# Unread products of eight columns on TensorE, at the start of a DeltaNet and feed-forward kernel

## The chip, the cores and the metric

The kernel runs on one core of a Trainium2 chip. A core has a matrix engine (TensorE, PE in the profile, with its weight loads shown as PEld), a vector engine (DVE), a scalar engine (ACT), a general engine (GpSimd, POOL) and a queue engine that issues transfers (SP). They work side by side and wait for each other through semaphores. Each of them carries out its own list of instructions in order; the list lies in memory, and an instruction queue brings it to the engine (q8 in the profile for TensorE). The metric is the device time of one launch in microseconds.

## The reference

Two layers stand one behind the other. The first is a delta rule over a sequence, for 4 batches and 8 heads, 768 steps and a head size of 48; the second is a feed-forward layer with exact GELU on 3072 tokens, 384 columns and 2048 hidden columns.

```python
k_n = k / (np.linalg.norm(k, axis=-1, keepdims=True) + 1e-06)
for t in range(S):
    y[:, :, t] = q_t @ state
    v_old = state.T @ k_t
    state = state + beta_t * outer(k_t, v_t - v_old)
x = y.transpose(0, 2, 1, 3).reshape(B * S, H * D)
h = x @ w_in
g = 0.5 * h * (1.0 + erf(h / sqrt(2)))
out = g @ w_out
```

All inputs are float32 but for the two weights of the feed-forward layer, which come as 64-bit floats and are decoded to 32 bits by the kernel.

## The kernel before

The sequence is cut into 12 chunks of 64 steps. A unit is one chunk of two batches (a = 0 or 1), with its 8 heads, so that 128 rows are filled: 64 steps of the one batch and 64 of the other. Inside a chunk the recurrence becomes a triangular system: K times K transposed, scaled by beta and by the norms of K, is eliminated in blocks of 32, the inverse is applied to V less the state's part, and the chunk's outputs and the next state follow from it.

The first four units (chunks 0 and 1, `first` in the code) are started by hand: within `by_hand` (L1201 to L1299) all five engines keep the order in which the code issues. For the work behind it a planner sorts the steps by due times written out in a list; there DVE and POOL keep that order, and PE keeps it where a chain of dependencies is laid.

What TensorE does in the part written by hand, in its order:

- For each of the four units, the transposition of K (L419, tile psT): four matmuls against the identity `ident`, after the unit's K has landed. ACT copies the result out as Kt (L420).
- In between and behind, the diagonal 32x32 products of K with itself (`diagonals`, L487, tile psD): 64 matmuls per unit in the profile's count, with 64 weight loads. The order is: transposition of unit 0, of unit 1, diagonals of unit 0, transposition of unit 2, diagonals of unit 1, transposition of unit 3, diagonals of unit 2, the signs of two chunks (L1195, psB, transpositions of beta), diagonals of unit 3. ACT copies each group out as `diag` (L489).
- The remaining products of K with itself (`grams`, L440, psG), once for each of the four units, and the signs of the other ten chunks.
- For each of the four units, the transposition of Q (L419 with `x` = 1), the copy by ACT, and then `queries` (L440, psG): Q times K transposed, which waits for that copy.
- The same for the units of chunks 2 and 3, then joins, solves and so on.

A float32 product appears in the profile as two weight loads and two matmuls, a transposition as one of each.

DVE meanwhile computes the norms of K (L345, L346), their roots (L390 to L396) and the factors from beta and the norms (L324 to L328), turns the factors (L498), turns all four units' diagonals at once (`flip`, L508), scales them (L513, with XM, which POOL made from the turned factors at L501) and eliminates row by row (L523 to L530). Then come the turns back (L539, L543), the joins of the 32x32 blocks (L578 on PE, L589 on DVE) and the decoding of the first weights (L255 to L282).

PSUM tiles come from pools by tag. The tag "mlp" has two buffers that are used in turn; the first tiles with it in the kernel before are `psY` of the first unit (L811), used behind the elimination.

## Time and profile before

| | us |
|---|---|
| median of 3 runs | 625.35 |
| the runs | 626.43, 625.1, 625.35 |
| the profiled execution | 626.68 |
| its span, first to last instruction | 624.9 |
| PE busy in it | 602.5 (96%) |
| DVE busy | 440.1 (70%) |
| ACT busy | 241.4 (39%) |
| POOL busy | 212.6 (34%) |

The span is cut into stretches by the views of the profile; times in them are microseconds from its start. A group of matmuls in the timeline is written with its line, output and input tiles, its shape, and its count. Brackets at the end of a row hold the idle time of the engine ahead of the group, and what ended it: another engine's instruction, a transfer, or "issue", which is time in which the engine waited for nothing that the profile shows. The chain that ended last is followed back from the last instruction: at each step to what released it, or to the instruction before it on the same engine. The row PEclk gives the granted TensorE clock as a share of the full one; the matmuls' own durations can be read beside it.

### The profile page before, as it was taken

How to read it: one execution, taken by the hardware profiler on the slowest of the kernel's cores; microseconds unless marked ns; L12 is line 12 of the kernel's file. 1: busy time of each engine (PE TensorE's matmuls, PEld its weight loads, DVE VectorE, ACT ScalarE, POOL GpSimd, SP SyncE). 2: the span in 40 equal slices, each digit the busy share in tenths (PEclk: the TensorE clock that was granted, in tenths of full speed). 3: DMA queues.
4: the chain of work that ended last, by engine and by line, in shares of the span. 5: the costliest groups of instructions: out<-in, count | busy, mean ns of one | idle time of the engine just before them, and what ended most of it. 6: DMA issues, size and time to landing. Idle time of an engine off the chain costs nothing.

```text
span 624.9 us, 19704 instructions
## 1 busy us (share of the span) xinstructions
PE 602.5 (96%) x8358; PEld 537.7 (86%) x8358; DVE 440.1 (70%) x811; ACT 241.4 (39%) x546; POOL 212.6 (34%) x316
## 2 busy tenths in 40 slices
PE   5768999999999999999999999999999999999997
PEld 4657786776899998998899998899998899988997
DVE  6999899999967697774859755859745947332532
ACT  3576877625443264224451134451134222044200
POOL 4045002100379821687222885222885200000000
PEclk9996999999999999999999999999999999999999
DMA  9793775002423452353123533013421001010011
GB/s 134 164 294 118 174 179 149 17 10 40 72 38 49 77 93 37 57 115 39 16 43 55 95 70 39 13 29 52 79 50 17 12 3 27 3 24 1 0 27 26
DMA packets 159576, 39.64 MB, mean 63 GB/s; under 512 B 151168, under 2 KB 154368, under 8 KB 159488
## 3 DMA queue, kind: packets, MB, share of 16 engines
q1 hardware_dynamic: 156816, 37.34, 30.9%
q10 hardware_dynamic: 2672, 1.03, 0.9%
q8 instruction: 66, 1.08, 0.7%
q14 instruction: 22, 0.18, 0.1%
HBM read 33.62 MB, written 4.72 MB: 61 GB/s over the span
## 4 chain that ended last, share of the span: by engine, by line
PE 81%; DVE 14%; issue 2%; DMA 1%; ACT 1%; SPq 0%; DVEq 0%
PE psX L966 13%; PE psY L1032 11%; PE psY L966 9%; PE psX L1032 9%; PE psV L1032 6%; PE psZ L1032 6%; PE psZ L966 4%; PE psV L966 4%; DVE tmp L528 3%; DVE Nu L530 3%; PE psK L732 3%; PE psO L933 3%; PE psH L915 2%; PE psY L822 2%; PE psU L792 2%
## 5 line engine op out<-in xcount | busy, mean ns | idle before, releaser
L377 POOL TENSOR_TENSOR n<-n,half 128x16 f32<-128x16 f32 x10 | 31.4, 3138 | 180.1 <-DVE n L375 130.0
L530 POOL TENSOR_TENSOR Nu<-Nu,tmp 128x30 f32<-128x30 f32 (+14 forms) x120 | 65.0, 541 | 9.4
L528 POOL TENSOR_TENSOR tmp<-Nu 128x30 f32<-128x30 f32 (+14 forms) x120 | 62.4, 520 | 9.4
L1032 PE MATMUL psX<-xT,w_in_sb 128*128 128x256 f32 (+1 forms) x288 | 62.6, 346 | 0.0
L966 PE MATMUL psX<-w_out_sb,G 128*128 128x192 f32 x320 | 56.1, 329 | 0.0
L966 PEld LDWEIGHTS psX<-w_out_sb,G 128*128 128x128 f32 x320 | 52.2, 190 | 0.7
L1032 PEld LDWEIGHTS psX<-xT,w_in_sb 128*128 128x128 f32 x288 | 47.9, 190 | 5.4
L915 PE MATMUL psH<-xT,w_in_sb 128*128 128x256 f32 x192 | 44.7, 387 | 0.7 <-ACT G L1015 0.5
L933 PE MATMUL psO<-w_out_sb,G 128*128 128x384 f32 x128 | 43.9, 490 | 0.0
L851 DVE TENSOR_TENSOR V<-psY,y 64x192 f32<-64x192 f32 (+1 forms) x60 | 21.3, 355 | 31.0 <-PE psY L834 27.0
L915 PEld LDWEIGHTS psH<-xT,w_in_sb 128*128 128x128 f32 x192 | 36.2, 192 | 7.9 <-ACT G L1015 2.3
L1060 DVE TENSOR_TENSOR psY<-psY,pu 128x512 f32<-128x512 f32 x20 | 14.0, 700 | 40.5 <-PE psY L1032 39.9
L1032 PE MATMUL psY<-xT,w_in_sb 128*128 128x256 f32 (+1 forms) x192 | 41.5, 345 | 0.0
L1015 ACT COPY xT<-psX 128x768 f32<-128x768 f32 x9 | 7.2, 799 | 79.8 <-PE psX L892 79.8
L1015 ACT COPY pu<-psZ 128x512 f32<-128x512 f32 x40 | 23.5, 587 | 37.3 <-PE psZ L1032 35.0
L933 PEld LDWEIGHTS psO<-w_out_sb,G 128*128 128x128 f32 x128 | 23.6, 190 | 14.1
L1032 PEld LDWEIGHTS psY<-xT,w_in_sb 128*128 128x128 f32 x192 | 32.1, 191 | 3.5
L1015 ACT ACTIVATE G<-G 128x512 f32<-128x512 f32 x40 | 25.2, 631 | 21.0 <-DVE G L1068 20.8
L1068 DVE TENSOR_TENSOR G<-psY,pu 128x512 f32<-128x512 f32 x20 | 13.8, 691 | 22.2 <-PE psY L1032 21.5
L1015 ACT ACTIVATE G<-psY 128x512 f32<-128x512 f32 x20 | 11.9, 596 | 45.3 <-PE psY L1032 45.3
L966 PE MATMUL psY<-w_out_sb,G 128*128 128x192 f32 x160 | 28.1, 329 | 0.0
L966 PE MATMUL psZ<-T,pu 128*128 128x192 f32 x160 | 28.1, 329 | 0.0
(207 smaller groups left out, 1370.2 us busy)
## 6 DMA issues: line engine op xcount, KB each, us to landing
Kp<-in_k_dram SPq DMA_DIRECT2D x76, 96.0 KB, 3.2
w_out_sb<-in_moe_w_in_dram SPq DMA_DIRECT2D x24, 256.0 KB, 4.0
V<-in_v_dram SPq DMA_DIRECT2D x48, 96.0 KB, 3.1
w_raw<-in_moe_w_out_dram SPq DMA_DIRECT2D x12, 384.0 KB, 7.4
out_dram<-o_sb SPq DMA_DIRECT2D x40, 96.0 KB, 2.2
Qp<-in_k_dram SPq DMA_DIRECT2D x64, 32.0 KB, 2.3
G<-in_moe_w_out_dram SPq DMA_DIRECT2D x4, 384.0 KB, 5.1
Qp<-in_q_dram SPq DMA_DIRECT2D x96, 16.0 KB, 2.0
```

What stands on the lines that cost most here:

```text
L377: nc.gpsimd.tensor_tensor(flat, flat, half, op=ALU.pow)
L528: rows_on.tensor_tensor(tmp, nu[:, j + 1:, j:j + 1].to_broadcast([128, n, j]), nu[:, j:j + 1, 0:j].to_broadcast([128, n, j]), op=ALU.mult)
L530: rows_on.tensor_tensor(nu[:, j + 1:, 0:j], nu[:, j + 1:, 0:j], tmp, op=ALU.add)
L732: nc.tensor.matmul(u.psK[HALF[p], r, j, :], lhsT=u.Kt[rows, p, j, :], rhs=SQ[rows, u.a, p ^ r, j, 0:w], start=True, stop=True)
L851: nc.vector.tensor_tensor(dst, src, pairs(u.y[at_], s), op=ALU.add)
L915: nc.tensor.matmul(psH, lhsT=w_in_sb[:, f // 2, m, f % 2 * 128:(f % 2 + 1) * 128], rhs=xTs[c][:, m, :], start=(m == 0), stop=(m == NM - 1))
L933: nc.tensor.matmul(u.psO, lhsT=G[:, u.a, f, :], rhs=w_out_sb[:, f, :], start=(f == 0), stop=(f == NF - 1))
L966: nc.tensor.matmul(ps_, lhsT=lhs[:, f, :], rhs=rhs[:, f, :], start=first and f == 0, stop=f == FH - 1, skip_group_check=not first)
L1015: i = fn(*args, **kw)
L1032: nc.tensor.matmul(ps_[:, i], lhsT=lhs[:, f // 2, f % 2 * 128:(f % 2 + 1) * 128], rhs=rhs, start=first and i == 0, stop=True, skip_group_c ...
L1060: nc.vector.tensor_tensor(L1["Y1"], L1["Y1"], L1["pu"][:, 0], op=ALU.add)
L1068: nc.vector.tensor_tensor(half(1, 1), shaped(L1["Y1"]), shaped(L1["pu"][:, 0]), op=ALU.add)
```

## The change

A helper `unread` is added. It takes a tile with the tag "mlp" and issues n products of a 32x8 slice of the identity with the same slice, all into the same 8x8 corner of that tile. Nothing reads the tile. Each product has 8 weight columns and 8 moving columns over 32 rows and is two weight loads and two matmuls. The helper is called with 38 ahead of the loop over the first units, so ahead of the first transposition of K, and with 4 in each of the four rounds of the loop that transposes Q, between the transposition and `queries`. That makes 54 products, 216 instructions, all on TensorE. Nothing else is changed.

```diff
+    def unread(n):
+
+        psI = ps.tile([128, 512], F32, tag="mlp", name="psI")
+        for _ in range(n):
+            nc.tensor.matmul(psI[0:H, 0:H], lhsT=ident[0:HB, 0:H], rhs=ident[0:HB, 0:H],
+                             start=True, stop=True)
+
...
         ns[c] = n0[:, c * NA:(c + 1) * NA]
+    unread(38)
     for u in first:
         squares(u, n0[:, u.t], nc.gpsimd if u.t == 1 else nc.vector)
         transposed(u, (0,))
...
         if u.c == 1:
             for x in sums_[5 * u.a:5 * u.a + 5]:
                 sum_of_squares(*x)
+        unread(4)
         queries([u])
     for a in range(NA):
         fetch_q(tiles[2, a])
```

## The prediction

> **What bounds the kernel now.** I read the page first: its slices and the chain that ended last.

> ```profile
> span 624.9 us, 19704 instructions
> ...
> PEclk9996999999999999999999999999999999999999
> ...
> q8 instruction: 66, 1.08, 0.7%
> ...
> PE 81%; DVE 14%; issue 2%; DMA 1%; ACT 1%; SPq 0%; DVEq 0%
> ```

> PE carries 81% of the chain, DVE 14%. Then I read busy time by stretches, to see where each of them does so (columns: stretch, length, then busy time with counts of PE, PEld, DVE, ACT, POOL, then clock and DMA).

> ```profile
> 67.00:150.00 83.00, 82.46 (x920) 62.39 (x918) 77.05 (x142) 49.87 (x140) 4.79 (x2) 1.00 0.35 85
> 150.00:240.00 90.00, 89.99 (x1547) 82.17 (x1540) 72.05 (x121) 38.50 (x79) 49.11 (x71) 1.00 0.42 66
> 240.00:250.00 10.00, 8.98 (x231) 8.50 (x230) 6.24 (x14) 4.48 (x9) 2.75 (x1) 1.00 0.25 32
> 250.00:350.00 100.00, 100.00 (x1612) 91.65 (x1615) 73.30 (x133) 34.71 (x71) 51.68 (x76) 1.00 0.34 56
> ```

> From 67 us on PE hardly ever stands still, so the end moves with the time at which PE gets there and with any stop after it. The one large stop is the 1.02 us at 240 to 250. Before 67 us the chain lies on DVE: from the flip of the diagonals (L508) at 14.95, through the elimination, to the join for which PE waits at 66.87. The change sits ahead of this, so the start of the chain matters:

> ```profile
> 12.01 0.27 PE psD L487 x10
> 12.28 1.36 issue
> 13.63 0.90 PE psD L487 x46
> ...
> 14.55 0.38 ACT diag L489
> ...
> 14.95 1.98 DVE Nu L508
> ```

> PE stands still for 1.36 us in the middle of the fourth group of diagonal products, waiting for no semaphore. DVE had been ready before the flip, since its previous instruction ended at 13.85:

> ```profile
> 13.64 0.21 DVE L498 STREAM_TRANSPOSE gt<-gm 128x32 f32<-128x32 f32 x1
> 14.95 1.97 DVE L508 STREAM_TRANSPOSE Nu<-diag 128x1024 f32<-128x1024 f32 x1 [1.10 <-ACT diag L489]
> ```

> So at most 1.1 us can be won there. PE's timeline tells what the stop is:

> ```profile
> 11.94 0.34 PE L487 MATMUL psD<-Kt 48*32 48x32 f32 x10
> 13.63 0.80 PE L487 MATMUL psD<-Kt 48*32 48x32 f32 x54 [1.36 <-issue]
> 14.37 2.40 PE L440 MATMUL psG<-Kt 48*64 48x64 f32 x74
> 17.37 1.76 PE L440 MATMUL psG<-Kt 48*64 48x64 f32 x54 [0.60 <-issue]
> ```

> **The change, part by part.** *38 products ahead of the first transposition.* A product is two weight loads and two matmuls, so 152 instructions. No row has this shape. Per load and matmul the nearest are psB (128 weight and 32 moving columns), 1.27 us for 10 or 127 ns; psJ at the same slow pace (32 and 32, two row groups in turn), 1.95 for 64, so 60 in each group; psD, four tiles at once, 14. A straight line through the first two gives 27 ns for 8 and 8 columns; bounds 14 and 127. 76 pairs take 2.05 us (1.1 to 9.7). They wait only for the identity, ready at 1.48, and so end at about 3.6; the first transposition waits for its K load until 4.47. Its price is nothing; if that cover went (127 ns) they would end at 11.2.

> *Four products behind each transposition of Q.* 8 pairs, 0.22 us, in the 0.67 us for which PE waits for ACT's copy (four gaps between 21 and 31). Hidden; without the cover 0.9 us of PE in a stage where DVE's elimination runs until 39.6 and PE idles another 2.06 us before 38.10. Nothing. No DMA, ACT, DVE, POOL or SP instruction is added or moved. The five unread tiles take turns with other "mlp" tiles, first used at 50.5 by PE itself: nothing.

> *What moves: the block edges.* With 152 instructions in front, the edges fall at the old numbers 41, 297 and 553 instead of 193, 449 and 705; with all 216, that of 7617 falls at 7401 and 7657.
> Number 41 stands in the first diagonal group, at 7.09. By the first fetch's 4.62 us (same loads under way) its block is there at 11.71; number 297, the beginning of the third group, was run at 10.76, so that group starts 0.95 late. Crossing there asks for the block of 553; between the rows 4.62 and 3.73 I take the middle, 4.18, because the loads thin out at 13 us. It is there at 15.89. Number 553 is the first instruction of the very last product of the fourth group (553 to 556), which the rest reaches at about 13.7. The flip began 0.80 after number 553 (14.15 to 14.95), so it now begins at 16.69: **1.74 later**. With 3.73 twice it is 0.40 later, with 4.62 twice 2.18. The other input of the elimination, the factors, is only 0.3 late (the signs move from 11.58 to 12.5) and stays ahead. What is late next is DVE's whole elimination, the decode behind it, and PE's join at 66.87; PE idles only 0.36 and 0.48 in that stretch, so I pass on all of it.

> *The late stop.* The new edges 7401 and 7657 are 242.56 and 246.05 (247.07 less the stop): 3.49 us apart, against 4.04 in the row. But the request runs ahead behind slow matmuls: between 4033 and 4289, another pair of edges, only 2.71 us passed without a stop, and eight slow matmuls stand ahead of 7381. I take 0.2 us of stop as left, **0.82 won**; bounds 0 and 1.02.

> *Sum.* +1.74-0.82=+0.92; ends +0.40-1.02=-0.62 and +2.18. The profiled execution took 626.68 (span 624.9 and 1.78 around it) and would take 627.60; it lies 1.33 above the median, 625.35, which becomes 626.27 (624.73 to 627.53).

> **Rivals.**
> *Faster: the last product comes in time.* If the edge falls at least four instructions later, or its block arrives by 12.6, only the third group is late: without any stop the fourth would end at 14.20-1.59=12.61, now at 13.56, and the flip starts at 14.31, 0.64 earlier; with the late stop's 0.82, 623.89. It decides at four instructions. For it: a single product is cut off. Against it: my count is exact at three stops.
> *Slower: new stops later.* Stretches of 256 that now begin at an edge and pass quickest are 7913 to 8169 (2.11 us) and 9449 to 9705 (2.10). If the request does not run ahead there, each costs 4.04-2.1=1.9: one makes 628.2. Slow matmuls stand ahead of both, which speaks against it.
> *The products are slow.* At 127 ns the first transposition moves from 4.47 to 11.2 and the second by 5: about 630.
> *Nothing moves:* PE has room for more, and the stops have another cause: 625.35.
> *The clock.* The slices give full clock in the first 34 us, but 48x64 matmuls last 315 ns there and 64x48 ones 308 in the stage at 0.50, against 220 behind 60 us: PE is slow until about 34. If the products woke it, number 41 would come up to 0.5 earlier and the end at 625.8; the blocks would still be waited for. [...]

> **How the numbers follow.** About 0.2% (1.25 us) is what a measurement of this kernel can tell from no change. Forecast 0.48 (0.27 of it within 0.2%, 0.21 slower, as its range goes to 627.53); faster rival 0.22 (0.20 faster, 0.02 within); new stops 0.12; slow products 0.05; nothing 0.08; clock 0.05. That makes 0.20 faster, 0.42 within, 0.38 slower. The time is the forecast's, 626.27. The range reaches to the faster rival and past the forecast's upper end towards the new stops: 623.7 to 628.0.

> **What would show it.** PE: 76 pairs end near 3.6; a stop before the third diagonal group and another two pairs ahead of the end of the fourth; L508 near 16.7; the join near 68.6; no 1.0 us stop at 245. Wrong, if L508 starts before 14.95, if stops keep their old matmuls, or if PE stops after 67 us where it did not.

## The result and the profile after

The changed kernel takes 628.06 us (median of 6 runs, 626.82 to 628.61), the kernel before 625.63 us beside it (6 runs, 625.1 to 626.43). The ratio is 1.0035, with a 95% interval of 1.0022 to 1.0048: slower by 0.35%, or 2.2 us (1.4 to 3.0). The prediction had +0.92 us, a ratio of 1.0015: the direction was right, the size less than half of what was measured. It gave a slowdown of more than 0.2% a chance of 0.38, less than the 0.42 for a time within 0.2%. Its range, 623.7 to 628.0, was set on the median of 625.35 known then; by the ratio the changed kernel stands at 627.5 on that base, inside the range, while the median of 628.06 lies just past its end.

The profiled execution of the changed kernel took 626.82 us, only 0.14 more than the 626.68 of the kernel before: it is the quickest of its runs, and that of the kernel before lies above all six of the runs beside it. So one pair of profiles hides most of the difference, and below three profiles of each kernel are read side by side. First the page of the changed kernel (span; granted clock in 40 slices; TensorE's instruction queue with packets, MB and share; the chain that ended last).

```profile
span 625.1 us, 19920 instructions
...
PEclk9985999999999999999999999999999999999999
...
q8 instruction: 66, 1.08, 0.7%
...
PE 80%; DVE 15%; issue 2%; ACT 1%; DMA 1%; SPq 0%; DVEq 0%
```

There are 216 instructions more and the same 66 packets. Then the busy time by stretches (PE, PEld, DVE, ACT, POOL with counts, then clock, DMA share and GB/s).

```profile
67.00:150.00 83.00, 82.36 (x876) 61.99 (x878) 77.05 (x142) 49.88 (x140) 4.79 (x2) 1.00 0.36 86
150.00:240.00 90.00, 90.00 (x1588) 82.19 (x1580) 71.95 (x122) 38.49 (x79) 48.91 (x70) 1.00 0.41 67
240.00:250.00 10.00, 10.00 (x240) 9.64 (x239) 6.28 (x13) 5.11 (x12) 2.90 (x1) 1.00 0.24 31
250.00:350.00 100.00, 99.31 (x1594) 90.90 (x1595) 74.19 (x134) 34.68 (x71) 51.44 (x75) 1.00 0.34 56
```

The 1.02 us that PE stood still between 240 and 250 are gone. In the next stretch, which was full, 0.69 us have come up. The start is read in PE's timeline of the changed kernel.

```profile
1.53 2.05 PE L1205 MATMUL psI<-ident 32*8 32x8 f32 x76 [1.53 <-POOL ident masks.py:199]
4.32 1.09 PE L419 MATMUL psT<-ident,Kp 128*128 128x128 f32 x4 [0.73 <-DMA Kp<-in_k_dram]
...
11.31 0.88 PE L487 MATMUL psD<-Kt 48*32 48x32 f32 x64 [0.41 <-issue]
12.12 0.42 PE L1195 MATMUL psB<-ident,w_in_sb 32*128 32x32 f32 x2
12.47 0.88 PE L487 MATMUL psD<-Kt 48*32 48x32 f32 x62
14.88 0.32 PE L487 MATMUL psD<-Kt 48*32 48x32 f32 x2 [1.53 <-issue]
```

The 76 pairs take 2.05 us and end ahead of K, which PE still waits for. The third group of diagonals (x64) starts behind a stop of 0.41, and the fourth is cut into 62 matmuls and 2: its last product alone waits for 1.53 us. The chain that ended last, of the same kernel, runs through that cut and on into DVE.

```profile
12.54 0.81 PE psD L487 x52
13.35 1.53 issue
14.88 0.33 PE psD L487 x2
...
15.23 0.38 ACT diag L489
...
15.64 1.96 DVE Nu L508
```

DVE's timeline says what the flip (L508) had to wait for. It was ready at 13.92, and ACT's copy of the cut group kept it for 1.72 us, where it was 1.10 before.

```profile
13.71 0.21 DVE L498 STREAM_TRANSPOSE gt<-gm 128x32 f32<-128x32 f32 x1
15.64 1.95 DVE L508 STREAM_TRANSPOSE Nu<-diag 128x1024 f32<-128x1024 f32 x1 [1.72 <-ACT diag L489]
```

Behind 244 us PE's timeline of the changed kernel has no stop in the products of L834 (that with 21 and 11 matmuls before), but a wait for DVE seven microseconds later.

```profile
244.40 0.54 PE L834 MATMUL psY<-V,Kp 64*48 64x48 f32 x32
...
251.77 1.76 PE L732 MATMUL psK<-SQ,Kt 48*64 48x112 f32 x64 [0.69 <-DVE SQ L841]
```

### The profile page after: what moved, and what is told of

Its sections match the earlier page's. It is cut to its first block, busy times and chain, and to the rows that moved or that the text cites. A ratio compares the mean times of both kernels' runs of the same rounds, so it can differ in the third digit from the quotient of the medians.

```text
span 625.1 us, 19920 instructions
## 1 busy us (share of the span) xinstructions
PE 609.2 (97%) x8466; PEld 544.2 (87%) x8466; DVE 440.6 (70%) x811; ACT 241.1 (39%) x546; POOL 212.4 (34%) x316
## 3 DMA queue, kind: packets, MB, share of 16 engines
q8 instruction: 66, 1.08, 0.7%
## 4 chain that ended last, share of the span: by engine, by line
PE 80%; DVE 15%; issue 2%; ACT 1%; DMA 1%; SPq 0%; DVEq 0%
PE psX L966 12%; PE psY L1032 11%; PE psY L966 9%; PE psX L1032 9%; PE psV L1032 6%; PE psZ L1032 6%; PE psV L966 4%; PE psZ L966 4%; DVE Nu L530 3%; DVE tmp L528 3%; PE psK L732 3%; PE psO L933 3%; PE psH L915 2%; PE psU L792 2%; PE psQ L752 2%
## 5 line engine op out<-in xcount | busy, mean ns | idle before, releaser
L851 DVE TENSOR_TENSOR V<-psY,y 64x192 f32<-64x192 f32 (+1 forms) x60 | 21.3, 355 | 30.4 <-PE psY L834 26.4
L933 PEld LDWEIGHTS psO<-w_out_sb,G 128*128 128x128 f32 x128 | 23.6, 190 | 14.1
```

The source lines that it names most:

```text
L851: nc.vector.tensor_tensor(dst, src, pairs(u.y[at_], s), op=ALU.add)
L933: nc.tensor.matmul(u.psO, lhsT=G[:, u.a, f, :], rhs=w_out_sb[:, f, :], start=(f == 0), stop=(f == NF - 1))
```

## The experiments

Four moments are compared throughout, each from one profiled execution: the start of the flip (L508); the join that PE waits for near 67 us (L578, psJ from Zf and XM); the products psK (L732) near 251, from their first weight load, as their distance from that join; and the end of the last matmul, as its distance from psK. "New stop" names a stop of PE that waits for no semaphore and that the kernel before does not have, by the number of the recorded PE instruction. Ratios are to the kernel before, run beside each; one without a ratio ran once.

| kernel | ratio, 95% interval | profile | flip | join | psK less join | end less psK | new stop behind 67 us |
|---|---|---|---|---|---|---|---|
| before | 1 | 626.68 | 14.95 | 66.86 | 184.69 | 369.89 | - |
| before again (e5) | 1.0004, 0.9992 to 1.0016 | 628.62 | 14.32 | 66.43 | 187.19 | 369.85 | - |
| before, third (e11) | - | 626.07 | 14.16 | 66.62 | 184.38 | 369.91 | - |
| after | 1.0035, 1.0022 to 1.0048 | 626.82 | 15.64 | 67.58 | 184.16 | 369.93 | none |
| after again (e1) | 1.0040, 1.0026 to 1.0055 | 628.69 | 16.85 | 68.65 | 184.19 | 370.68 | 8385: 0.67 |
| after, third (e10) | - | 628.77 | 16.95 | 68.80 | 184.23 | 370.55 | 8385: 0.54 |
| only the 38 (e2) | 1.0053, 1.0034 to 1.0072 | 629.38 | 16.70 | 68.62 | 184.36 | 371.21 | 9921: 1.15 |
| only the fours (e3) | 1.0016, 1.0005 to 1.0027 | 626.97 | 14.42 | 66.55 | 184.15 | 371.11 | 12481: 1.05; 7617, now ahead of L822: 0.31 |
| 37 and fours (e4) | 1.0017, 1.0005 to 1.0030 | 625.83 | 14.35 | 66.71 | 184.22 | 369.74 | none |
| only 64 (e6) | 1.0008, 0.9998 to 1.0017 | 626.64 | 15.22 | 67.13 | 184.44 | 369.91 | none |
| 54 behind Q (e7) | 1.0048, 1.0029 to 1.0067 | 628.43 | 14.14 | 68.50 | 184.21 | 370.56 | 8385: 0.54 |
| 18, fours, 19 (e8) | 1.0004, 0.9994 to 1.0014 | 627.48 | 15.65 | 67.89 | 184.20 | 370.22 | 8385: 0.21 |
| 54 in idle time (e9) | 1.0027, 1.0018 to 1.0037 | 627.77 | 14.60 | 67.85 | 184.20 | 370.55 | 8385: 0.54 |

**Both kernels again (e1 and e5, e10 and e11).** No edit.

> The changed kernel once more, for a second profile. Block edges: the fourth group of diagonal products is again cut ahead of its last product (62 and 2 matmuls), the flip L508 starts at 15.6 and the join for which PE waited starts 0.7 later than before. The median of the changed kernel lay 1.2 above its own profiled execution; if this profile is a slower execution, the theory of the clock (PE stays at half clock into the stage of 57 to 62 us and comes late to the join) expects the missing 1.2 us between 49 and 70 us, with no idle PE ahead of the join; a theory of late stops expects idle PE behind 70 us. Ratio to before 1.003 to 1.005.

> The kernel before once more, for a second profile and a check of the comparison itself. Ratio 1.000. Block edges: stops ahead of the recorded instructions 449, 705 and 7617 again, with other lengths, since the time from crossing to restart was between 3.6 and 4.9 us in the runs so far; the flip L508 between 14.2 and 15.2. Its first profile was 0.7 above the median of before, so this one should have a shorter early stop.

> The changed kernel a third time, for the spread of its early edges. Flip 15.6 to 16.9 with the join 52 behind it; stops at recorded 705 and 961 with a crossing to restart between 3.2 and 4.9. If its flip falls within 14.1 to 15.0, the difference between the two kernels at the flip is no more than scatter.

> The kernel before a third time. Flip 14.1 to 15.0, join 66.4 to 66.9, stops at recorded 449 and 705 and, of 0.4 to 1.0, at 7617. If its flip falls at 15.6 or later, the difference between the two kernels at the flip is no more than scatter.

The third profile of the changed kernel, PE's timeline from 11 us:

```profile
11.54 0.92 PE L487 MATMUL psD<-Kt 48*32 48x32 f32 x64 [0.41 <-issue]
12.39 0.42 PE L1195 MATMUL psB<-ident,w_in_sb 32*128 32x32 f32 x2
12.74 0.87 PE L487 MATMUL psD<-Kt 48*32 48x32 f32 x62
16.20 0.31 PE L487 MATMUL psD<-Kt 48*32 48x32 f32 x2 [2.59 <-issue]
```

The same of the kernel before, its third profile:

```profile
12.02 0.27 PE L487 MATMUL psD<-Kt 48*32 48x32 f32 x10
13.04 0.67 PE L487 MATMUL psD<-Kt 48*32 48x32 f32 x54 [0.75 <-issue]
13.64 1.73 PE L440 MATMUL psG<-Kt 48*64 48x64 f32 x74
17.86 1.76 PE L440 MATMUL psG<-Kt 48*64 48x64 f32 x54 [2.50 <-issue]
```

The stops keep their place to the instruction (62 and 2, 10 and 54, 74 and 54), and their length changes from execution to execution: 1.53, 2.36 and 2.59 us ahead of the same last product in the three profiles of the changed kernel. The two sets of flips do not overlap: 14.16 to 14.95 before, 15.64 to 16.95 after. The means are 14.48 and 16.48, so the changed kernel's flip is 2.0 us late. The join's means are 66.64 and 68.34: 1.7 us late. Both are above the scatter of either kernel, 1.3 us at most, so they are no accident of one profile.

**One part alone (e2 and e3).** e2 has the 38 products only, e3 the four in each round only.

```diff
+    unread(38)          # e2 alone
     for u in first:
         squares(u, n0[:, u.t], nc.gpsimd if u.t == 1 else nc.vector)
...
+        unread(4)       # e3 alone
         queries([u])
```

> Only the 38 products ahead of the first transposition. Block edges: the early stage is that of the changed kernel, L508 at 15.6 (0.7 later than before). The late edges fall 152 off, at 7465 and 7721 of the old count, so the stop at 244 us goes, and others may come where 256 instructions now pass in 2.1 to 2.9 us from edge to edge (5417, 6953, 9513, 12073 of the old count): 626 to 628. If the 16 products behind the transpositions of Q are what costs (their own time, or the clock), it is back at before, 625.6.

> Only the products behind the transpositions of Q. Block edges: the early stage is that of before, with the stop of 1.36 us at 12.28 and L508 at 14.95; the late edges fall 64 off, at 7553, and the 256 instructions ahead of it pass in 2.85 us, so a stop of about 1 us stays: 625.6, within 0.5 of before. If these products cost by themselves: the changed kernel's 628.

The whole early loss belongs to the 38: flip 16.70 and join 68.62 with them alone, 14.42 and 66.55 with the fours alone. The fours cost nothing where they stand. But both kernels are slower than before, and than expected: 629.58 us at the median for e2, where at most 628 was expected, and 627.22 for e3 beside 625.96 of the kernel before, from which it was to stay within 0.5. Each has a new stop late in the kernel. That of e2 ends one of the four quick stretches that its expectation named (9513 of the old count and the 256 behind it); for e3 none was foreseen, and the stop expected near 244 us shrank to 0.31. In the timeline of e2 it parts one group of products:

```profile
321.05 0.80 PE L440 MATMUL psG<-Kt 48*64 48x64 f32 x37
323.00 0.68 PE L440 MATMUL psG<-Kt 48*64 48x64 f32 x27 [1.15 <-issue]
```

and in that of e3 another:

```profile
411.56 0.92 PE L440 MATMUL psG<-Kt 48*64 48x64 f32 x44
413.53 0.56 PE L440 MATMUL psG<-Kt 48*64 48x64 f32 x20 [1.05 <-issue]
```

Both lie at 193 plus a multiple of 256 (9921 and 12481). The end less psK is longer by 1.3 and 1.2 us, the length of these stops and little more.

**A whole block (e6).** 64 products, 256 instructions, ahead of the first transposition and nothing else, so that every edge falls on the instruction it fell on before.

```diff
+    unread(64)
     for u in first:
         squares(u, n0[:, u.t], nc.gpsimd if u.t == 1 else nc.vector)
```

> 64 products ahead of the first transposition and none behind Q: 256 instructions, exactly one block. Block edges: all stops keep their old matmuls (the 11th pair of the fourth diagonal group, number 128 of the following products with K, the 22nd of the products at 244 us), and the time is that of before within 0.5 us, although more products are issued than in the run with 38, which took 629.6. If the products themselves, or the clock that they wake, cost time, it is as slow as with 38 or slower: 629 or more.

PE's timeline of e6 has the stops of the kernel before, at the same cuts of 10 and 54, and 74 and 54:

```profile
1.53 3.35 PE L1205 MATMUL psI<-ident 32*8 32x8 f32 x128 [1.53 <-POOL ident masks.py:199]
...
10.15 0.63 PE L419 MATMUL psT<-ident,Kp 128*128 128x128 f32 x4
...
13.96 0.81 PE L487 MATMUL psD<-Kt 48*32 48x32 f32 x54 [2.01 <-issue]
14.70 2.39 PE L440 MATMUL psG<-Kt 48*64 48x64 f32 x74
18.52 1.77 PE L440 MATMUL psG<-Kt 48*64 48x64 f32 x54 [1.43 <-issue]
```

With ten more products in front than the changed kernel has in all, the time is 1.0008 (0.9998 to 1.0017) of that before. So it is neither the products' own time nor their number that costs the changed kernel its 2 us, but where they put the edges. The run bears on the clock too. The records have the clock at full from 9.88 to 13.29 here, and the transposition at 10.15 takes 0.63 us instead of 1.11. That the products woke it is not shown: in the third profile of the kernel before, which has none, it rose at 11.63. It gained nothing, as PE then stood still for 2.01 us at the next edge.

**One product less (e4).** 37 in front instead of 38, the fours kept: the edge falls four instructions later and spares the fourth group's last product. This is the prediction's faster rival, made on purpose.

```diff
-    unread(38)
+    unread(37)
```

> 37 instead of 38 products ahead, the 16 behind Q kept. Block edges: the third edge falls right behind the last product of the fourth group, so of the two early stops only the one ahead of the third group (0.4 us) delays the flip: L508 at 13.9 to 14.2 instead of 15.64, so 1.4 to 1.7 us less than the changed kernel, about 626.5, and L440 stops in its place. If the cut last product is not what delays the flip, it is like the changed kernel, 628.

PE's timeline of e4:

```profile
11.87 0.87 PE L487 MATMUL psD<-Kt 48*32 48x32 f32 x62 [0.73 <-issue]
12.67 0.42 PE L1195 MATMUL psB<-ident,w_in_sb 32*128 32x32 f32 x2
13.02 0.89 PE L487 MATMUL psD<-Kt 48*32 48x32 f32 x64
16.53 3.69 PE L440 MATMUL psG<-Kt 48*64 48x64 f32 x128 [2.62 <-issue]
```

The four instructions decide as the prediction said: the fourth group is whole, and the flip starts at 14.35, 2.1 us ahead of the changed kernel's mean. But this does not make the kernel faster than before: 1.0017 (1.0005 to 1.0030). The stop of 2.62 us now stands ahead of `grams`, and PE's own way to the first join becomes the late one. DVE has its turned half ready at 41.46, but PE, held up by its own products, comes only at 42.75, 28.4 us behind the flip. In the changed kernel, where DVE is the late one, it comes 27.2 to 27.5 behind it. In the second and third profile of the kernel before, with stops of 1.43 and 2.50 us ahead of the same products, it is 28.2 and 28.4: an early flip is of use only as far as PE keeps up with it. The profile shown is the second quickest of twelve runs (625.58 to 629.09), so where the other 1.5 us up to its median of 627.29 go was not seen.

**The late part without the early one (e7, e9) and the products spread (e8).** e7 issues all 54 behind the loop over Q. e9 keeps the fours and places 19 ahead of the transpositions of chunk 3's K, where PE idled 2.06 us, and 19 between the two joins, where it idled 1.49. e8 has 18 in front, the fours, and 19 ahead of those transpositions.

```diff
         queries([u])
+    unread(54)                 # e7 alone
...
+    unread(19)                 # e8, e9
     for u in fourth:
         transposed(u, (0,))
...
         join(0, (a,), 0)
+    unread(19)                 # e9 alone
     back2[0](*back2[1:])
```

> The same 54 products all behind the stage of Q, ahead of nothing that waits for the elimination: the early stage is that of before, the later edges are those of the changed kernel. Block edges: the flip at 14.2 to 15.2 as in before, from the join to the last matmul 554.1 to 554.9 as with the changed kernel (before 554.6), no stop at 244 but the wait of 0.66 us for DVE near 251: 625.5 to 626.5. If the 216 instructions cost wherever they stand: 628.

> All 54 products, so the same shift of 216 instructions for everything behind the first four units, but none ahead of the diagonals, and none where they make a chain late: 16 behind the transpositions of Q, 19 into the idle 2.06 us ahead of 38.10 and 19 into the idle 1.49 us between the two joins. So the early edges lie as in the kernel before. Theory of the early edges: flip (L508) at 14.1 to 15.0, join 66.4 to 66.9. For the late part two rivals. As predicted (only the 1.0 us stop at 244 goes): join to last matmul 486.9 where the kernel before had 487.7 in its first profile, time 0.5 to 0.9 below the kernel before. As the profiles of the shifted kernels so far read (a wait of 0.66 for DVE at 251 takes its place, and a stop of 0.2 to 0.7 at old number 8169): join to last matmul 486.5 to 487.9, time within 0.4 of the kernel before.

> 18 products ahead of the first transposition, 4 behind each transposition of Q, 19 ahead of the transpositions of K of chunk 3, where PE idles 2 us: 212 instructions in all, as with 37. Block edges: the early edges fall at 121, 377 and 633 of the old count; number 377 was run at 11.2 and its block is there at 11.6 to 12.2, so the fourth diagonal group ends 0.5 to 1.0 later than without any stop, and the flip starts at 13.9 to 14.5, while the products behind it are held up less than with 37. The time is 0.5 to 1.0 below before: 625.0 to 625.5. If edges do not matter here: 627 to 628.

The distances from the join in the expectation of e9 have the join's own time, 66.86, taken off twice. With it added, they read 553.8 for the prediction, against 554.58 in the first profile before, and 553.4 to 554.8 for the rival.

The flips of e7 and e9 are early (14.14 and 14.60), since their early edges are those of the kernel before. Their late part is that of the changed kernel's third profile to 0.03 us: psK 184.21 and 184.20 behind the join, the end 370.56 and 370.55 behind psK. The sum in e9, 554.75, is the rival's upper end, not the prediction's 553.8: in spite of the stop of 244 us being gone, nothing is won behind the join.

Both also have the join late, against what was expected. In e7 the 108 pairs last 2.85 us on PE, which idled only 1.25 us ahead of the first join in the first profile before, and DVE waits. Its median of 629.25 us, where 625.5 to 626.5 was expected, would by itself fit the rival that 216 instructions cost wherever they stand; e6 with 256 of them and e8 with 212, both level with the kernel before, speak against that rival. DVE's timeline of e7:

```profile
45.28 0.86 DVE L589 TENSOR_TENSOR XM<-psJ,gm 32x256 f32<-32x256 f32 x2 [2.08 <-PE psJ L578]
```

In e9 an edge falls among the 19 products between the joins. PE's timeline of e9:

```profile
47.17 0.82 PE L1205 MATMUL psI<-ident 32*8 32x8 f32 x27 [1.90 <-issue]
```

That edge was crossed at 41.26 and PE went on at 47.17, 5.9 us later; e3 has a stop at the same number with 5.7. So the second join begins 4.9 us behind the first, not 2.7, and the last join 1.2 us late. e8 equals the kernel before, 1.0004 (0.9994 to 1.0014), where 0.5 to 1.0 us less was expected. Its flip is not at 13.9 to 14.5 but at 15.65, because the stop inside the third group lasted long. PE's timeline of e8:

```profile
13.60 0.44 PE L487 MATMUL psD<-Kt 48*32 48x32 f32 x24 [1.85 <-issue]
```

From the crossing at 7.79 to this restart passed 5.8 us, where the two early edges of the other profiles took 3.6 to 4.9. The profile is at the upper end of its runs (626.3 to 627.48). No version was found that beats the kernel before.

**Why the late stop was worth so little.** The profile of before answers it. DVE's timeline, kernel before:

```profile
245.12 0.69 DVE L1099 TENSOR_TENSOR pu<-G 128x512 f32<-128x512 f32 x1 [3.57 <-ACT G L1015]
...
249.84 1.12 DVE L841 TENSOR_TENSOR SQ<-SQ,psY 48x384 f32<-48x384 f32 x2
```

and the changed kernel:

```profile
245.78 0.69 DVE L1099 TENSOR_TENSOR pu<-G 128x512 f32<-128x512 f32 x1 [3.57 <-ACT G L1015]
...
250.51 1.12 DVE L841 TENSOR_TENSOR SQ<-SQ,psY 48x384 f32<-48x384 f32 x2
```

DVE's work towards SQ starts from ACT's G, which PE had fed before it stopped at 244.17, and then runs on DVE with no gap over 0.04 us. The products that the stop delays end at 245.57, ahead of 246.45, when DVE first reads a psY in this work (L851). So PE's stop never reaches it. In the first profile before, SQ is ready at 250.96 and psK starts at 251.55: no more than 0.59 of the 1.02 could be won. SQ is ready 184.10 us behind the join with a stop of 1.02, 184.06 with 0.75 (e11), and 184.04 without one. So psK cannot start earlier than some 184.2 behind the join, and in the kernel before it started at 184.69 and 184.38. The stop of 1.02 cost 0.5 us and that of 0.75 cost 0.2; the rest was time that PE would have waited for DVE.

## Why the prediction was right or wrong, point by point

- **PE runs out of instructions, in blocks of 256, at fixed numbers.** Right. Each idle time of PE that a timeline of the thirteen profiles puts down to issue lies at 193 plus a multiple of 256, with new places as the count moves, and at the old instruction again when it moves by a whole block (e6). The one exception is that of 1.56 to 1.88 us ahead of psU (L792) near 48 us, which the profiles of e2, e3 and e9 put down to POOL's Zf (L560). The stops fit a PE that has the block it is in and the next: where it stopped, it went on 2.9 to 6.2 us after it had crossed into the block ahead of the one it waited for.
- **76 pairs at 27 ns, hidden.** Right: 2.05 us, ended at 3.58 ahead of K. The first transposition starts at 4.32, 4.54 and 4.48, against 4.45 to 4.47 before.
- **Four products behind Q, 0.22 us, hidden.** Hidden, and a little dearer: eight matmuls last 0.35 us in the timeline, and the idle time ahead of `queries` goes from 0.67 to 0.39.
- **The third group 0.95 late, at 11.71.** Right in kind and a little high: it starts at 11.31, 11.70 and 11.54, since the first crossing took 4.15, 4.44 and 4.15 us instead of 4.62, from 7.15, 7.26 and 7.39. In the second profile the row names ACT's Kt (L420) as what ended this stop, but that copy, begun at 11.04, is the fourth unit's; the third unit's had ended at 9.77.
- **The last product cut off, flip at 16.69, +1.74.** Right, as a mean over executions: flip 15.64, 16.85 and 16.95, mean 16.48. The second crossing took 3.57, 4.39 and 4.66, where 4.18 was assumed. The base was less good than the step: the profile shown of before had the latest flip of its three, so that against the means the flip moved by 2.0.
- **DVE's elimination passes all of it on to the join.** Right but for 0.3: the join lies 51.8 to 51.9 us behind the flip in the changed kernel and 51.9 to 52.5 before, where PE is late for the first join in two profiles. The join moved by 1.71, for 1.74 predicted. That these two agree so closely is luck: the flip moved by 0.3 more than predicted, and 0.3 of it was not passed on.
- **The late stop, -0.82.** This step failed, twice. First, the stop of 1.02 was counted in full, but half of it covered a wait for DVE: psK less the join gets shorter by 0.34 on the means (184.54 of the two undisturbed profiles before, 184.19 after). The prediction names what is late next for the early part only. Had it followed DVE's row at 245.12, released by ACT, it would have found this bound in the profile of before. Second, the stop did not only go: in two of the three profiles another came at a new edge, behind 67 us, where PE had not stopped before. That is one of the prediction's own signs of being wrong.
- **The rival of new stops later, 1.9 us each.** It came in part, at the one of its two edges that the old numbers 7913 to 8169 named (8385 with the 216 in front): 0.67 and 0.54 us in two of the three profiles, none in the first, and nothing at the other edge. The prediction took these for its two quickest stretches; old numbers 12521 to 12777 pass in 1.92 us, quicker than either, and no stop came there. A third of the price, because PE went on 3.0 to 3.1 us behind the crossing instead of the 4.04 of the row taken. PE's timeline of the third profile of the changed kernel shows it:

```profile
262.16 0.43 PE L966 MATMUL psX<-T,G 128*128 128x192 f32 x1
263.13 2.71 PE L966 MATMUL psX<-T,G 128*128 128x192 f32 x15 [0.54 <-issue]
```

- **The sum.** Predicted +1.74 and -0.82. On the means of the profiles: +1.71 to the join, -0.34 from there to psK and +0.50 behind it, so +1.87 at the last matmul, where the runs have +2.2 (1.4 to 3.0). The late part is +0.16 instead of -0.82, and that is the size of the miss.
- **The faster rival.** Its decision point, four instructions, was right (e4). Its price was not: the flip came early, but PE became late for the first join, and the kernel was not faster.
- **Slow products, nothing moves.** Neither: the 76 pairs took 2.05 us, and the stops came ahead of other instructions when the count moved by 216 or by 152. **The clock:** the products of the changed kernel did not wake it; its first rise is at 37.24, 38.78 and 39.06 us, later than in any profile of before (34.24, 35.62 and 11.63). In e6, with 3.35 us of products and the transpositions behind them, it rose at 9.88. But in the third profile of the kernel before it rose at 11.63 without any products, in the first two not until 34.24 and 35.62 with the same work, so what raises it no run here settles.

## What to carry to other kernels

When an engine stands still for nothing that the profile shows, number its recorded instructions: stops a multiple of a fixed number of instructions apart, here 256, point to block edges, and whatever adds or takes away instructions moves every later one, so price the places where edges arrive as well as those that they leave. Before counting an engine's idle time as a gain, follow the other inputs of its next waiting instruction and see when each was ready; here half of a stop was cover for a wait on another engine. And where a wait's length varies from one execution to the next, one profile of each kernel is too little to size a difference of 0.3%.

## What the runs showed that was not expected

- The time from a crossing to PE's going on varies between executions of the same kernel at the same instruction: at the two early edges of the changed kernel 4.15, 4.44, 4.15 and 3.57, 4.39, 4.66 us, in the kernel before 4.62, 4.06, 3.78 and 3.73, 4.55, 4.82. Over all kernels it lay between 2.9 us (near 262 us, e8) and 6.2 us (near 52 us, e3). Why it varies was not tried.
- An early rise of the clock gained nothing ahead of an edge in the two profiles that have one, e6 and the third of the kernel before. In the latter the clock was full from 11.63 to 15.04 us, and 74 products of `grams` took 1.73 us instead of 2.39; PE then stood still for 2.50 us, where it had been 0.60.
- In the second profile of the kernel before (e5), PE idled 1.17 us ahead of 139.34, waiting for DVE, and the granted clock fell to half from 141.44 to 144.85, for 3.41 us. psK came 187.19 us behind the join there, 2.5 to 2.8 more than in the other two, so the later distances of that profile are left out of the means.
